# Zero regions of two gradients: stored from SBUF, or copied from memory to memory

## The chip, the cores and the metric

The kernel runs on one core of one Trainium2 chip. The metric is the device time of one execution in microseconds (us). Several executions are timed, and the median counts. Smaller is better.

## The reference

The reference is one step of a decoding layer and all of its gradients. With batch 4, one token, model width 512, it computes

- `xn = layernorm(x)`;
- attention of 32 query heads over 8 groups of cached keys and values. The cache has 4096 positions, and only the last `W = 1024` of them are used (`k_cache[:, :, Sk - W:, :]`);
- a feed-forward part of width 1792, `(gelu(xn @ w_gate) * (xn @ w_up)) @ w_down`;
- the output `x + attention + feed-forward`, and with `jax.vjp` the gradients for x, the two caches, and the five weight matrices, for a given `grad_out`.

The gradients of the two caches, `out_2` (keys) and `out_3` (values), have the caches' full shape, 4 x 8 x 4096 x 128 in bf16. The window leaves the first 3072 of the 4096 positions unused, so three quarters of these two outputs are zeros: 4 x 8 x 3072 x 128 x 2 bytes = 25.2 MB in each, 50.3 MB together. They must be written all the same.

## The kernel before, in words

The program is written for the engines in a fixed order: each engine runs its instructions as the source issues them. Almost all DMAs are issued by SP (`nc.sync`), in one queue. ACT issues one load at the start and the two small outputs at the end, and POOL issues the later weight loads.

*Stages.* First the small inputs are loaded, then the feed-forward weights, the first attention weights `wo` and `wq`, and the first blocks of keys (`kb`) and values (`vb`). The feed-forward part is computed and its weight gradients are made piece by piece. Then a loop over `t` runs through four stages (`NT = 4`), each with two groups of the cache. A stage transposes key and value blocks, forms scores and softmax (`kv_steps`, `softmax`), forms the softmax's gradient (`softmax_d`), multiplies back (`odq`), sums up (`fin`), and loads what the stage after the next one needs (`load_kv`, `load_w`).

*Pieces in the background.* The gradients of caches and weights are cut into short closures. They lie in a queue, `bg`, and `tick(n)` runs the next n of them between the steps of a stage. A piece of the cache gradients (`dvdk`) is one matmul and a copy from PSUM to a staging tile (`stg_dv`, `stg_dk`, three buffers). The last piece of a tile issues the tile's store and after that calls `zero()`. The pieces of the weight gradients stage in `osb_d`, `osb_g`, `osb_o` and `osb_q`, four buffers.

*Zeros.* `ztile` is an SBUF tile of 128 x 6144 bf16 that POOL fills with zeros at the start (L167). `zlist` lists 32 regions, 16 in each of the two outputs; a region is the unused part of two groups (`ZR = 2`) of one batch element, 2 x 768 KB = 1.573 MB. `zero(n)` takes the next n regions and stores `ztile` to each. Calls of `zero` are spread over the program: three at the start (L168), some with the feed-forward gradients, one after each cache gradient tile, four in the last stage, and what is left at the end.

*Stores.* All stores go through `store`, which declares that stores of the kinds "rest" and "zeros" write disjoint parts, so that no waits are made between them:

```
for k in ("rest", "zeros") if kind == "rest" else ("rest",):
    tc.declare_no_dep(d.ins, group=k, reason="stores write disjoint parts of the outputs")
tc.add_to_no_dep_group(kind, d.ins)
```

All the stores have one line in the profile, L103, and are told apart by their tiles. DMA completions use eight semaphores in turn, so a DMA on SP waits for the landing of the one issued eight places earlier.

Of the kernel before, what the change touches and what calls it, by code (L numbers as in the profile page):

```python
# [14 lines left out]
P = 128  # L15
# [3 lines left out]
def kernel(  # L19
# [28 lines left out]
    nc = tc.nc  # L48
# [7 lines left out]
    K0 = Sk - W  # L56
# [43 lines left out]
    def store(eng, out, in_, kind):  # L100

        eng.nop()
        d = eng.dma_start(out=out, in_=in_)  # L103
# [3 lines that stand above are left out]
        return d  # L107
# [48 lines left out]
    ZR = 2  # L156
    ZW = K0 * Dh * ZR // P
    ztile = const.tile([P, ZW], BF16, name="ztile")
    zlist = deque((og, b, g) for b in range(B) for g in range(0, G, ZR) for og in (out_2, out_3))

    def zero(n=1):
        for _ in range(min(n, len(zlist))):
            og, b, g = zlist.popleft()
            store(nc.sync, og[b, g:g + ZR, 0:K0, :].rearrange("g (m j) d -> m g (j d)", m=P // ZR), ztile[:], "zeros")


    nc.gpsimd.memset(ztile[:], 0.0)  # L167
    zero(3)  # L168
    ident_f = const.tile([P, P], FP32, name="ident_f")
    nc.vector.tensor_copy(out=ident_f[:], in_=ident[:])  # L170
# [304 lines left out]
    def dvdk(t, k):  # L475
        src, mr, og = st[t][("P", "dS")[k]], st[t][("do", "q")[k]], (out_3, out_2)[k]
        nm = ("dv", "dk")[k]

        def piece(g, j, held):
            if j == 0:  # L480
                held["stg"] = stage.tile([P, JB, Dh], BF16, name="stg_" + nm, tag="stg")
            stg = held["stg"]
            mps = ps_w.tile([P, NQ, Dh], FP32, name="kv_ps", tag="w")
            nc.tensor.matmul(mps[:].rearrange("p q d -> p (q d)"), lhsT=src[:, j * P:(j + 1) * P],  # L484
                             rhs=mr[:, g].rearrange("p q d -> p (q d)"), start=True, stop=True)
            evac(stg[:].rearrange("p (q j) d -> p j q d", q=NQ)[:, j], mps[:], 512)
            if j == JQ - 1:
                store(nc.sync, og[:, t * GP + g, K0:Sk, :].rearrange("b (m j) d -> m b (j d)", j=JB),
                      stg[:].rearrange("p j d -> p (j d)"), "rest")
                zero()  # L490

        made = []
        for g in range(GP):
            held = {}
            made.append([lambda g=g, j=j, held=held: piece(g, j, held) for j in range(JQ)])
        return made
# [158 lines left out]
    def piece_d(f4, i, n, held):  # L655
        if i == 0:
            held["osb"] = outp.tile([P, 4, D], BF16, name="osb_d", tag="o")
        m = n * P // 4
        mps = ps_w.tile([P, D], FP32, name="dwd_ps", tag="w")
        nc.tensor.matmul(mps[0:m], lhsT=a_s[:, f4].rearrange("p i f -> p (i f)")[:, i:n * P:4], rhs=dyr[:],  # L660
                         start=True, stop=True)
        evac(held["osb"][0:m, i, :], mps[0:m], 512)
        if i == 3:
            store(nc.sync, out_8[4 * f4 * P:(4 * f4 + n) * P, :].rearrange("(p i) n -> p (i n)", i=4),
                  held["osb"][0:m].rearrange("p i n -> p (i n)"), "rest")
            zero(f4 % 2)
# [151 lines left out]
```

## Time and profile before

| | |
|---|---|
| median of 3 runs | 282.77 us (282.73 to 283.42) |
| the profiled execution, its own time | 283.0 us |
| its span in the profile | 281.0 us |
| busy: PE, DVE, ACT, POOL | 203.1, 164.1, 117.8, 40.1 us |
| moved by DMA | 112.12 MB in 19565 packets |
| zero stores | 32 of 1536 KB, median 18.1 us from issue to landing |

The span is the time from the first to the last event of the profiled execution; its own time is somewhat longer, since it includes what lies around the span. PE is the matrix engine, DVE the vector engine, ACT the scalar engine; SPq is the queue of the engine that issues DMAs. A busy share belongs to the whole span, and stages differ. The time from issue to landing of a DMA includes the time that it stands in the queue behind others.

### The profile page before, as it was taken

How to read it: one execution, taken by the hardware profiler on the slowest of the kernel's cores; microseconds unless marked ns; L12 is line 12 of the kernel's file. 1: busy time of each engine (PE TensorE's matmuls, PEld its weight loads, DVE VectorE, ACT ScalarE, POOL GpSimd, SP SyncE). 2: the span in 40 equal slices, each digit the busy share in tenths (PEclk: the TensorE clock that was granted, in tenths of full speed). 3: DMA queues.
4: the chain of work that ended last, by engine and by line, in shares of the span. 5: the costliest groups of instructions: out<-in, count | busy, mean ns of one | idle time of the engine just before them, and what ended most of it. 6: DMA issues, size and time to landing. Idle time of an engine off the chain costs nothing.

```text
span 281.0 us, 6867 instructions
## 1 busy us (share of the span) xinstructions
PE 203.1 (72%) x2972; PEld 138.8 (49%) x2972; DVE 164.1 (58%) x313; ACT 117.8 (42%) x219; POOL 40.1 (14%) x40
## 2 busy tenths in 40 slices
PE   0276699959789889998999299898999599390000
PEld 0265476735456665566775156677556484140000
DVE  7946646645776655577666067767677728386000
ACT  2030386635035418764448056443866038370000
POOL 8600000007002150002250000223000400000000
PEclk9999589986999999999999969999999979977555
DMA  7999999999999999999999999999999999999990
GB/s 264 393 375 431 431 426 417 425 419 424 369 395 424 422 420 420 426 415 422 419 417 411 412 424 423 431 383 398 385 368 415 387 432 410 425 429 422 398 422 30
DMA packets 19565, 112.12 MB, mean 399 GB/s; under 512 B 1664, under 2 KB 4496, under 8 KB 11088
## 3 DMA queue, kind: packets, MB, share of 16 engines
q1 hardware_dynamic: 17744, 103.56, 89.6%
q0 software_dynamic: 1632, 6.29, 5.6%
q10 hardware_dynamic: 160, 1.84, 1.9%
q8 instruction: 23, 0.38, 0.5%
q14 instruction: 6, 0.05, 0.0%
HBM read 30.68 MB, written 81.01 MB: 397 GB/s over the span
## 4 chain that ended last, share of the span: by engine, by line
PE 47%; DMA 22%; DVE 16%; ACT 4%; issue 2%; SPq 0%; DVEq 0%; ACTq 0%
DMA out_dram<-stg_dv 13%; PE T_ps L279 8%; PE kv_ps L484 7%; DMA wd_sb<-in_B_w_down_dram 6%; PE S_ps L345 5%; PE od_ps L450 5%; DMA out_dram<-osb_g 4%; DVE T_sb L98 3%; DVE dS_s L367 2%; PE wdT_ps L279 2%; PE dwq_ps L520 2%; PE acc_ps L256 2%; PE dwd_ps L660 2%; DVE P_s L367 2%; PE wgT_ps L279 2%
## 5 line engine op out<-in xcount | busy, mean ns | idle before, releaser
L98 DVE COPY T_sb<-T_ps 128x1024 bf16<-128x1024 bf16 x64 | 44.1, 688 | 26.7 <-PE T_ps L279 26.5
L97 ACT CAST stg_dk<-kv_ps 128x512 bf16<-128x512 f32 x52 | 29.2, 588 | 31.2 <-PE kv_ps L484 12.4
L97 ACT CAST stg_dv<-kv_ps 128x512 bf16<-128x512 f32 x51 | 28.1, 588 | 24.9 <-PE kv_ps L484 24.3
L484 PE MATMUL kv_ps<-qmr,dS_s 128*128 128x512 bf16 x64 | 23.9, 414 | 11.3 <-ACT stg_dk L97 10.6
L463 POOL TENSOR_TENSOR o_s<-od_r,msk_r 128x512 bf16<-128x512 bf16 x8 | 9.1, 1157 | 110.2 <-DVE od_r L455 80.9
L484 PE MATMUL kv_ps<-domr,P_s 128*128 128x512 bf16 x64 | 21.3, 382 | 0.0
L279 PE MATMUL T_ps<-ident,vb 128*128 128x128 bf16 x256 | 20.3, 225 | 0.4 <-DVE T_sb L98 0.4
L279 PE MATMUL T_ps<-ident,kb 128*128 128x128 bf16 x256 | 20.4, 225 | 0.0
L279 PEld LDWEIGHTS <-kb 128*128 128x128 bf16 x256 | 17.5, 101 | 4.5 <-issue 1.3
L279 PEld LDWEIGHTS <-vb 128*128 128x128 bf16 x256 | 17.2, 101 | 5.0 <-issue 3.2
L97 ACT CAST osb_q<-dwq_ps 128x512 bf16<-128x512 f32 x25 | 14.6, 587 | 8.3 <-PE dwq_ps L520 7.4
L329 POOL TENSOR_TENSOR domr<-r,msk 128x1024 bf16<-128x1024 bf16 x4 | 7.6, 1892 | 71.2 <-DVE r L326 65.1
L97 ACT CAST osb_g<-dwg_ps 128x512 bf16<-128x512 f32 (+1 forms) x25 | 12.3, 544 | 12.3 <-PE dwg_ps L673 6.3
L97 ACT CAST osb_o<-dwo_ps 128x512 bf16<-128x512 f32 x24 | 13.9, 586 | 4.5 <-PE dwo_ps L505 2.9
L98 DVE CAST stg_dk<-kv_ps 128x512 bf16<-128x512 f32 x12 | 8.0, 688 | 12.0 <-DMA out_dram<-stg_dv 11.2
L98 DVE COPY wgT<-wgT_ps 128x1024 bf16<-128x1024 bf16 x14 | 9.6, 686 | 6.8 <-PE wgT_ps L279 6.8
L345 PE MATMUL S_ps<-T_sb,qm 128*32 128x256 bf16 x128 | 12.7, 387 | 0.6 <-DVE T_sb L98 0.5
L345 PE MATMUL S_ps<-T_sb,dom 128*32 128x256 bf16 x128 | 12.7, 388 | 0.1
L505 PE MATMUL dwo_ps<-dyr,o_s 128*128 128x512 bf16 x32 | 12.4, 413 | 0.3 <-ACT stg_dk L97 0.2
L98 DVE COPY woT<-woT_ps 128x1024 bf16<-128x1024 bf16 x16 | 11.0, 686 | 2.7 <-PE woT_ps L279 2.3
L484 PEld LDWEIGHTS <-dS_s 128*128 128x128 bf16 x64 | 6.2, 101 | 12.2 <-issue 11.1
L520 PE MATMUL dwq_ps<-od_r,xnm 128*128 128x256 bf16 x64 | 11.6, 274 | 0.3 <-ACT osb_q L97 0.2
(188 smaller groups left out, 385.0 us busy)
## 6 DMA issues: line engine op xcount, KB each, us to landing
out_dram<-ztile SPq DMA_DIRECT2D x32, 1536.0 KB, 18.1
kb<-in_A_k_cache_dram SPq DMA_DIRECT2D x8, 1024.0 KB, 17.4
vb<-in_A_v_cache_dram SPq DMA_DIRECT2D x8, 1024.0 KB, 20.7
out_dram<-stg_dv SPq DMA_DIRECT2D x8, 1024.0 KB, 13.0
out_dram<-stg_dk SPq DMA_DIRECT2D x8, 1024.0 KB, 20.8
out_dram<-osb_o SPq DMA_DIRECT2D x8, 512.0 KB, 17.4
out_dram<-osb_q SPq DMA_DIRECT2D x8, 512.0 KB, 13.8
out_dram<-osb_g SPq DMA_DIRECT2D x8, 448.0 KB, 14.3
```

The lines of the kernel that those rows point to most:

```text
L97: return nc.scalar.copy(out=out, in_=in_)
L98: return nc.vector.tensor_copy(out=out, in_=in_)
L256: nc.tensor.matmul(ps[:, c, :], lhsT=lf(c), rhs=rhs, start=(k == 0), stop=(k == len(terms) - 1))
L279: nc.tensor.transpose(ps[:, i, :], a, ident[:])
L329: nc.gpsimd.tensor_tensor(out=mr[:].rearrange("p g q d -> p (g q) d"), in0=r4[:, k, :].unsqueeze(1).broadcast_to([P, SL, Dh]), in1=msk[:]. ...
L345: nc.tensor.matmul(ps[b * RB:(b + 1) * RB, :], lhsT=zt[:, b * GP + g, c0:c0 + RB], rhs=T_sb[:].rearrange("p (x b) -> p b x", b=B)[:, b, :] ...
L367: nc.vector.scalar_tensor_tensor(out=out[:], in0=src[:].unsqueeze(2).broadcast_to([P, WQ, B]), scalar=rr[:, 0:1], in1=mskb[:].unsqueeze(1) ...
L450: nc.tensor.matmul(od_ps[g * 32:g * 32 + B * rep, k, g, :], lhsT=cols[:, jj, g * NQ + q, :], rhs=blks[(t, g)][:, j, :], start=(j == 0), st ...
L463: nc.gpsimd.tensor_tensor(out=o_s[:, g], in0=rows[:, g].unsqueeze(1).broadcast_to([P, rep, Dh]), in1=msk_r[:].unsqueeze(2).broadcast_to([P ...
L484: nc.tensor.matmul(mps[:].rearrange("p q d -> p (q d)"), lhsT=src[:, j * P:(j + 1) * P], rhs=mr[:, g].rearrange("p q d -> p (q d)"), start ...
L505: nc.tensor.matmul(mps[:], lhsT=o_s[:, g].rearrange("p r d -> p (r d)")[:, i:rep * Dh:rep], rhs=dyr[:], start=True, stop=True)
L520: nc.tensor.matmul(mps[:, i].rearrange("p g d -> p (g d)"), lhsT=xnm[:, i2 * 2 + i, c * P:(c + 1) * P], rhs=dq_r[:].rearrange("p g d -> p ...
```

## The change

The first three calls store `ztile` as before. Each of the other 29 regions is written by a DMA from memory to memory: its source is the first zero region, `out_2[0, 0:2, 0:3072, :]`, which the first of the three stores has filled. The copies are issued by SP in the places of the stores that they replace. A region is described as 16 x 2 rows of 24,576 bf16, 48 KB each, where a store has 64 x 2 rows of 6144, 12 KB each. As the copies read what the first store has written, the first of them gets a wait for that store's landing.

```diff
     zlist = deque((og, b, g) for b in range(B) for g in range(0, G, ZR) for og in (out_2, out_3))
+    ZN = len(zlist)
 
     def zero(n=1):
+
         for _ in range(min(n, len(zlist))):
             og, b, g = zlist.popleft()
-            store(nc.sync, og[b, g:g + ZR, 0:K0, :].rearrange("g (m j) d -> m g (j d)", m=P // ZR), ztile[:], "zeros")
+            dst = og[b, g:g + ZR, 0:K0, :]
+            if len(zlist) >= ZN - 3:
+                store(nc.sync, dst.rearrange("g (m j) d -> m g (j d)", m=P // ZR), ztile[:], "zeros")
+            else:
+                store(nc.sync, *(x.rearrange("g (m j) d -> m g (j d)", m=16) for x in (dst, out_2[0, 0:ZR, 0:K0, :])), "zeros")
```

## Prediction, made before the changed kernel ran

> **What bounds the kernel now.** I read the time slices first, then the queue rows, then windows without compute, then the chain.
>
> The slices of the page (each figure is 1/40 of the span, 7 us; DMA is the busy share of the 16 engines in tenths, GB/s what they moved):
>
> ```profile
> span 281.0 us, 6867 instructions
> ...
> DMA  7999999999999999999999999999999999999990
> GB/s 264 393 375 431 431 426 417 425 419 424 369 395 424 422 420 420 426 415 422 419 417 411 412 424 423 431 383 398 385 368 415 387 432 410 425 429 422 398 422 30
> DMA packets 19565, 112.12 MB, mean 399 GB/s; under 512 B 1664, under 2 KB 4496, under 8 KB 11088
> ## 3 DMA queue, kind: packets, MB, share of 16 engines
> q1 hardware_dynamic: 17744, 103.56, 89.6%
> q0 software_dynamic: 1632, 6.29, 5.6%
> ...
> HBM read 30.68 MB, written 81.01 MB: 397 GB/s over the span
> ```
>
> The DMA row is full from the second slice to the last but one and the rate is flat near 420 to 430 GB/s. PE is busy 72% of the span, DVE 58%. So the 16 DMA engines set the time, and engine gaps are mostly results of it. Two windows confirm this (busy us and counts per engine, then clock, DMA share, GB/s):
>
> ```profile
> 22.00:37.00 15.00, 9.95 (x157) 7.85 (x155) 9.31 (x24) 4.41 (x8) 0.00 (x0) 0.67 1.02 432
> ...
> 266.00:272.00 6.00, 0.00 (x0) 0.00 (x0) 0.00 (x0) 0.00 (x0) 0.00 (x0) 0.50 1.04 432
> ```
>
> The first holds loads of 8 KB rows and zero stores of 12 KB rows, the second the last zero stores, with no compute at all. Both give 432 GB/s: the same ceiling for reads from and writes to HBM, so it lies in what both share, the engines or the SBUF side. The chain of waits names the same resource: its largest line is a store's landing, and the largest single piece a stage buffer's store waiting in the DMA queue:
>
> ```profile
> DMA out_dram<-stg_dv 13%; PE T_ps L279 8%; PE kv_ps L484 7%; DMA wd_sb<-in_B_w_down_dram 6%; PE S_ps L345 5%; PE od_ps L450 5%; DMA out_dram<-osb_g 4%; DVE T_sb L98 3%; DVE dS_s L367 2%; PE wdT_ps L279 2%; PE dwq_ps L520 2%; PE acc_ps L256 2%; PE dwd_ps L660 2%; DVE P_s L367 2%; PE wgT_ps L279 2%
> ```
>
> In order of time (start, duration, what):
>
> ```profile
> 137.81 23.51 DMA out_dram<-stg_dv
> ```
>
> **Prices out of the queue rows.** q1 used 0.896 x 16 x 281.0 = 4,028 engine-us for 17,744 packets and 103.56 MB; q0 0.056 x 16 x 281.0 = 252 for 1,632 and 6.29 MB. Solved for a price per packet and one per byte: 12.8 ns and 36.7 ns per KB (27.2 GB/s per engine, 435 for 16). Rounding of q0's 5.6% leaves 9 to 17 ns per packet. A zero store has 128 rows of 12.288 KB, 8 per engine: 8 x (12.288 x 36.7 + 12.8) = **3.71 us** of all engines. 32 of them are 119 us of the span, 50.3 of 112.1 MB.
>
> **What the Trainium skill says.** (1) "DMA: Bandwidth & Descriptors", Where 436 GB/s comes from: 16 SBUF ports of 27.2 GB/s, and these ports are the bottleneck. The trace agrees in size: 432. A memory-to-memory copy doesn't use these ports. (2) "HBM Reference", Specifications (TRN2): a domain has about 716 GB/s, shared by two cores. A copy reads and writes each byte there, so it can't go over 358. The trace of before can't show it: its total is 397, each byte crossing HBM once. (3) "Collectives: The Full Stack", the section on the fold count: about 31 GB/s per engine, measured in ring copies between cores. No row of before tests it. (4) "DMA: Bandwidth & Descriptors", Queues, rings and completion order: each engine changes between queue rows only at packet ends. A packet of 48 KB thus holds up q0 longer than one of 12.
>
> **The change, part by part.**
>
> 1. *29 of 32 zero stores become copies.* The compiled order on SP's queue is the same, each copy in its store's place (16x2x24576 elements: 32 rows of 49.15 KB, two per engine, so still all 16 engines). Bytes over the engines don't change, 29 x 1.573 = 45.6 MB. HBM reads rise from 30.7 to 76.3 MB, all traffic at HBM from 111.7 to 157.3.
>    - *At the old engine rate* a copy takes 2 x (49.15 x 36.7 + 12.8) ns = 3.63 us, 0.08 less for 96 fewer packets: 29 x 0.077 = **-2.2 us** (-1.6 to -3.0 by the packet price).
>    - *At the domain's ceiling.* At 27.2 GB/s per engine it would draw 2 x 435 = 870 GB/s, more than 716. At 358 a copy takes 4.39 us: 29 x (4.39 - 3.71) = +19.9 us. I take 350, an estimate just below that ceiling[...]: 4.49 us, 29 x 0.78 = **+22.7 us**. Mixed traffic may cost more: at 300 GB/s it is 5.24 us, +44.5.
>    - *Cover.* The 16 engines may be apart, some in a copy while others move SBUF data; then HBM's demand averages out (157.3 MB / 716 = 220 us, below the span) and the loss shrinks. The trace shows how far apart: at the end the rate falls off within about 3 us, less than a copy lasts. So I count little cover; half of it would leave about +10.
>    As the DMA row has no idle slice, a longer copy isn't hidden; it goes in full to the end.
>
> 2. *The added wait.* The first copy now waits for the landing of the first zero store, its source. That was issued at 18.5 us and landed 21.8 later (the trace's answer on ztile for that issue), at 40.3; the copy's issue in before is at 40.8, behind two osb_d stores. I take 0, with 2 us as the bound if landing slips. Behind it on SP stand the osb_d and osb_g stores, for which ACT's next staging buffers wait; the DMA backlog (landings of 10 to 26 us for zero stores) covers such a slip. Later copies have the same one-semaphore waits as the stores they replace.
>
> 3. *Longer packets beside POOL's loads.* wo and wq for the next stages come on q0, 17 packets per engine and MB. A copy gives them 2 turns where a store gave 8. The first pair is issued at 67.6 and used from 88.3, landing after 13 to 22 us: tight, so PE may wait some us there. The later pairs (100.7 to 129.6, 142.5 to 179.0) have room. While PE waits, SP's backlog keeps the engines working: 0 taken, 3 us as the bound.
>
> 4. *SP's issue time.* A zero store took SP 0.66 us (median), one per 9 us. A copy describes 32 rows a side instead of 128: between 0.66 less and no gain, and nothing on the path since the queue is full. The first three stores, ztile and its memset stay. No other queue's order moves.
>
> Sum against the profiled execution (283.0 us, 2.0 around its span): 283.0 + 22.7 + 0 + 0 = 305.7. The median of the runs is 282.77, 0.2 below, so 305.5.
>
> **Rivals.**
> - *Engine rate kept (faster).* If HBM feeds both sides, or engines are well apart, only the packets count: 283 - 2 = 281. For it: HBM never showed a limit of its own. Against it: 870 of 716.
> - *The copy outruns the SBUF ports (faster).* Place: the 29 copies. At 31 GB/s per engine a copy takes 3.17 us, 29 x -0.54 = -15.7: 267. It decides from where a copy averages under 3.71 us, that is over 424 GB/s. For it: the ceiling of 432 may be the ports'. Against it: it needs 992 GB/s of HBM whenever all engines copy.
> - *Half rate (much slower).* If an engine can't read and write memory at once, 435 / 2 = 217: 7.25 us a copy, 29 x 3.54 = +103: 386. For it: no row shows both ends in HBM. Against it: the 31 GB/s of the skill.
> - *The rows don't stay long.* If the hardware cuts 48 KB rows to packets of 4 KB, there are 384 per copy, not 32: 29 x 352 x 12.8 ns / 16 = +8.2 on any of the above.
>
> **How the numbers follow.** HBM ceiling, 290 to 328: 0.55. Half rate or near it, above 328: 0.15. Mostly covered by engines apart, 282 to 290: 0.12, a third of it no change. Engine rate kept: 0.10. Outrun: 0.08. So faster by over 0.3% (0.85 us, about what can be told from no change) 0.18, within it 0.04, slower 0.78. Forecast 305.5. The range 278 to 352 leaves out most of the outrun case (0.07) and the slower part of half rate (0.10); its upper end is a copy rate of about 257 GB/s.
>
> **What would show it.** Right: 29 issues out_dram<-out_dram; HBM read near 76 MB; packets near 16,800; the slices sink in proportion to the copies in them, with DMA still at 9; the stretch after the last compute grows by some 1.5 us for its two copies. Engine rate kept: the last stretch stays at 432. Half rate: slices with copies near 250 to 300 and PE below 60%. Wrong altogether: idle slices in the DMA row, which would mean a wait (the first copy's, or PE's on wo near 88 us) and not a rate.

## The result and the profile after

The changed kernel takes **295.55 us** (median, 294.95 to 296.5) against 282.88 us for the kernel before in the same comparison (282.73 to 283.42): 12.7 us more, ratio 1.0447, 95% interval 1.0413 to 1.0482. The span of the profiled execution grew from 281.0 to 294.5 us.

The page of the changed kernel: slices (now 7.4 us each), queue rows and HBM line.

```profile
span 294.5 us, 6866 instructions
...
DMA  7999999999999999999999999999999999999892
GB/s 272 388 386 425 436 414 442 398 367 377 353 439 379 418 399 424 361 440 422 395 409 434 416 440 421 376 381 355 373 351 312 387 343 355 425 406 347 272 396 100
DMA packets 16781, 112.12 MB, mean 381 GB/s; under 512 B 1664, under 2 KB 4496, under 8 KB 11088
...
q1 hardware_dynamic: 14960, 103.56, 90.0%
...
HBM read 76.29 MB, written 81.01 MB: 534 GB/s over the span
```

The DMA row is as full as before. The same 112.12 MB went through the engines in 2,784 fewer packets, and it took them longer: the rate sinks to 312 to 390 in many slices. That is a lower rate, not a wait. The queue row gives the whole difference: q1's packets now took 0.900 x 16 x 294.5 = 4,241 engine-us where they took 4,028, that is 213 more, or 213 / 16 = **13.3 us** of all engines. The span grew by 13.5. The trace also records the start and the length of every packet. By these records 9.4 us of the growth lie in the zero regions' own packets; most of the rest, 3.1 us, lies in the packets of 8 KB, which took 329 ns in the mean instead of 317. So packets beside the copies became slower too.

Three windows of the changed kernel (busy us and counts of PE, PEld, DVE, ACT, POOL, then clock, DMA share, GB/s). The first lies ahead of the first copy, the second is the long middle part, the third lies after the last compute, where the final copies run:

```profile
22.00:37.00 15.00, 9.64 (x157) 7.46 (x155) 9.39 (x24) 4.49 (x8) 0.00 (x0) 0.64 1.02 430
...
42.00:280.00 238.00, 183.22 (x2588) 122.22 (x2585) 137.65 (x260) 105.50 (x201) 29.12 (x22) 0.91 1.00 388
...
274.00:285.00 11.00, 0.00 (x0) 0.00 (x0) 0.00 (x0) 0.00 (x0) 0.00 (x0) 0.50 0.97 340
```

The middle part of the kernel before, which ends earlier:

```profile
42.00:268.00 226.00, 179.75 (x2571) 119.62 (x2568) 136.63 (x259) 104.89 (x199) 29.12 (x22) 0.93 1.00 412
```

Ahead of the first copy nothing has changed (430 GB/s, 432 before). In the middle the kernel before moved 412 GB/s, now it is 388. In the tail it had 432, now 340, with the engines still busy 97% of the time. Engines that are as busy and move less have packets that take longer. Whether the engine itself is slower in a copy, or what it reads from and writes to, is for the experiments.

The loss doesn't lie evenly. Late in the program four zero regions are issued in a row (start, duration), as stores in the kernel before and as copies now:

```profile
219.74 4.40 SPq L103 DMA_DIRECT2D out_dram<-ztile  x4
...
225.40 2.94 SPq L103 DMA_DIRECT2D out_dram<-out_dram  x4
```

Up to there 19 copies had been issued and the changed kernel was 5.7 us behind, about 0.30 us per copy. At the end it was 13.5 us behind, so the last 10 copies, which mostly stand close to each other, go with 7.8 us, about 0.78 each. The packet records agree: copy packets that started from 80 to 210 us took 1.85 us in the mean, those from 210 us on 2.21.

The chain of waits passes the delay on through a larger share of DMA landings (39% of the span, 22% before):

```profile
DMA out_dram<-stg_dv 21%; DMA out_dram<-osb_o 9%; PE T_ps L285 6%; DMA wd_sb<-in_B_w_down_dram 5%; PE kv_ps L490 5%; DMA out_dram<-osb_g 4%; PE S_ps L351 4%; PE od_ps L456 4%; DVE T_sb L98 2%; PE dwq_ps L526 2%; PE wgT_ps L285 2%; PE dwd_ps L666 2%; PE wdT_ps L285 2%; PE dwg_ps L679 2%; PE acc_ps L262 1%
```

In the list of waits (us in total, times, longest) ACT stands longer before a staging tile whose last store hasn't landed, 16.1 us where it was 11.6:

```profile
ACT stg_dk L97 <- DMA out_dram<-stg_dv: 16.1, 2, 8.2
```

### The profile page after: what moved, and what is told of

It reads as the page before. It is cut to its first block, busy times and chain, and to the rows that moved or that the text cites. A ratio compares the mean times of both kernels' runs of the same rounds, so it can differ in the third digit from the quotient of the medians.

```text
span 294.5 us, 6866 instructions
## 1 busy us (share of the span) xinstructions
PE 206.2 (70%) x2972; PEld 141.1 (48%) x2972; DVE 164.5 (56%) x313; ACT 117.5 (40%) x219; POOL 40.1 (14%) x40
## 2 busy tenths in 40 slices
DMA packets 16781, 112.12 MB, mean 381 GB/s; under 512 B 1664, under 2 KB 4496, under 8 KB 11088
## 4 chain that ended last, share of the span: by engine, by line
DMA 39%; PE 35%; DVE 11%; ACT 3%; issue 2%; SPq 0%; DVEq 0%; ACTq 0%
DMA out_dram<-stg_dv 21%; DMA out_dram<-osb_o 9%; PE T_ps L285 6%; DMA wd_sb<-in_B_w_down_dram 5%; PE kv_ps L490 5%; DMA out_dram<-osb_g 4%; PE S_ps L351 4%; PE od_ps L456 4%; DVE T_sb L98 2%; PE dwq_ps L526 2%; PE wgT_ps L285 2%; PE dwd_ps L666 2%; PE wdT_ps L285 2%; PE dwg_ps L679 2%; PE acc_ps L262 1%
## 5 line engine op out<-in xcount | busy, mean ns | idle before, releaser
L97 ACT CAST stg_dk<-kv_ps 128x512 bf16<-128x512 f32 x52 | 28.9, 589 | 35.7 <-DMA out_dram<-stg_dv 16.1
L490 PE MATMUL kv_ps<-domr,P_s 128*128 128x512 bf16 x64 | 22.1, 393 | 2.8 <-DVE woT L98 1.8
L351 PE MATMUL S_ps<-T_sb,qm 128*32 128x256 bf16 x128 | 12.7, 387 | 0.6 <-DVE T_sb L98 0.5
L351 PE MATMUL S_ps<-T_sb,dom 128*32 128x256 bf16 x128 | 12.7, 387 | 0.1
L526 PE MATMUL dwq_ps<-od_r,xnm 128*128 128x256 bf16 x64 | 12.6, 301 | 0.1
```

What stands on the lines that cost most here:

```text
L97: return nc.scalar.copy(out=out, in_=in_)
L351: nc.tensor.matmul(ps[b * RB:(b + 1) * RB, :], lhsT=zt[:, b * GP + g, c0:c0 + RB], rhs=T_sb[:].rearrange("p (x b) -> p b x", b=B)[:, b, :] ...
L526: nc.tensor.matmul(mps[:, i].rearrange("p g d -> p (g d)"), lhsT=xnm[:, i2 * 2 + i, c * P:(c + 1) * P], rhs=dq_r[:].rearrange("p g d -> p ...
```

## The experiments

*The theory:* one core gets a limited supply from its HBM, reads and writes together. When all 16 engines copy at once they ask for twice their own rate, which is more than that; while some engines move SBUF data beside them, part of the loss is covered. *The rivals:* a copy costs each engine something by itself; the place of the source matters; one event (the added wait, a late weight load) costs the time; row length matters.

### Copies and stores alone

The isolated kernels keep only the filling of `ztile` and the DMAs of `zero`, called as `zero(32)`; everything else is left out. Each ran once, so their times have no interval, but the effects are several us and more.

All stores, none replaced:

```diff
-            if len(zlist) >= ZN - 3:
+            if True:
```

> Only the 32 zero stores from SBUF, back to back on SP; all other work is left out. Both theories: 32 x 3.71 = 118.7 us of data at some 430 GB/s plus a head (memset, first landing) and tail of about 15 us. This is the base for the isolated copies.

Three stores and 29 copies, as in the change:

> Only the 3 zero stores and the 29 copies, back to back on SP; all other work is left out. Theory (HBM's supply is the limit when all 16 engines copy, and in the full kernel about half of that loss is covered by engines that are apart): a copy alone costs more than the 4.2 us seen in the full kernel, near 4.5 us (350 GB/s), so some 22 us over the isolated stores. Rival (a copy has a fixed cost of its own, whatever stands beside it): the same 4.2 us as in the full kernel, some 13 us over the isolated stores.

Measured: 128.98 and **162.65 us**. The 29 copies cost 33.7 us more than stores, 1.16 each: a copy alone is dearer than in the full kernel (12.7 / 29 = 0.44), and dearer than I had expected (some 22 us over the stores). The windows of the two, stores first (POOL busy, clock, DMA share, GB/s):

```profile
20.00:110.00 90.00, 0.00 (x0) 1.00 1.01 424
```

```profile
20.00:150.00 130.00, 0.00 (x0) 1.00 1.00 325
```

With no other work and with full engines, stores run at 424 GB/s and copies at 325. A copy reads and writes each byte in HBM, so HBM then moves 650 GB/s.

### Fewer engines at a time

Each copy in two DMAs of 8 rows by 2:

```diff
-                store(nc.sync, *(x.rearrange(..., m=16) for x in (dst, ...)), "zeros")
+                for q in range(2):
+                    store(nc.sync, *(x.rearrange(..., m=16)[q * 8:q * 8 + 8] for x in (dst, ...)), "zeros")
```

> As the isolated copies, but each copy is cut into two DMAs of 8 rows by 2, so that each runs on 8 engines; all other work is left out. Theory (HBM's supply): 8 engines ask for 435 GB/s of HBM, well inside it, so each packet of 48 KB runs at the engine's own 1.82 us: 58 x 2 x 1.82 = 211 us for the copies, 217 GB/s. Rival (an engine loses time on each memory-to-memory row by itself): 2.1 to 2.3 us a packet, 244 to 267 us for the copies.

Measured: 233.69 us. Less the head and tail of the isolated stores (128.98 - 32 x 3.71 = 10.3) and three stores (11.1), 212.3 are the copies', where the theory said 211 and the rival 244 to 267.

```profile
40.00:200.00 160.00, 0.00 (x0) 1.00 0.50 216
```

Half of the engines are busy and move 216 GB/s: 27.0 each, the rate of an engine in the stores of the kernel before (432 / 16). So a memory-to-memory row has no price of its own here, in either direction: with eight engines copying an engine loses nothing, and it doesn't go beyond 27 GB/s though SBUF is at neither end. A packet of 48 KB took 1.815 us; with 16 engines it took 2.40 in the mean.

Twelve engines, by rows of 32 KB (`m=24`):

> Isolated copies (all other work left out) as 24 x 2 rows of 32 KB, so that only 12 of the 16 engines carry them. Theory (HBM's supply of some 646 GB/s): 12 engines ask for 12 x 2 x 27.1 = 650 GB/s, just what there is; each row runs near the engine's own 1.22 us and the total stays near the 162.65 us of 16 engines: 160 to 168 us. Rival (the loss is a share of each engine's own rate, or grows with the number of rows in flight): 4/3 of the copies' time, 200 us and more, or clearly less than the 16 engines' time.

Measured: 163.22 us; 16 engines had 162.65.

```profile
20.00:150.00 130.00, 0.00 (x0) 1.00 0.75 324
```

Twelve engines, each at its own full rate of 27.0 GB/s, move as much as sixteen. The last four add nothing: in a long run of copies the limit is outside of the engines. Whether it is the memory itself or the path to it, these runs don't tell apart; I call it HBM's supply.

### Another source

```diff
-(dst, out_2[0, 0:ZR, 0:K0, :])
+(dst, A_k_cache[b, g:g + ZR, 512:512 + K0, :])
```

> Isolated copies whose source is not the one zero region but another part of the key cache for each copy, shifted by 512 positions (128 KB) against its destination; the contents of the two outputs are thus not zeros, and all other work is left out. Theory (HBM's supply): no change, 160 to 165 us. Rival (the loss comes from reading the same 1.5 MB again and again, or from source and destination lying at the same place of a 2 MB grid): clearly faster, toward 134 us.

Measured: 162.67 us, to 0.02 us the same as with the one source. Neither reading one region 29 times nor the equal offsets of source and destination cost anything.

### The cover

Alternating stores and copies (`if len(zlist) >= ZN - 3 or len(zlist) % 2`: 15 copies, 17 stores):

> Isolated as before (all other work left out), but from the fourth region on every second one is a copy (15 copies, 17 stores from SBUF, alternating in SP's one queue). Theory (cover by engines that are apart: while some copy, others store, and HBM's demand averages to 1.5 x 427 = 640 GB/s, about the 646 that the isolated copies drew): nearly all of the loss of 1.16 us per copy goes, 129 to 137 us. Rival (a copy pays its 1.16 us wherever it stands): 128.98 + 15 x 1.16 = 146.4 us.

The same DMAs in two blocks (`if len(zlist) >= ZN - 17`):

> The 17 stores and 15 copies of the alternating isolated kernel in two blocks, all stores first and then all copies (all other work left out). Theory (in the alternating order the stores beside the copies cover half of the loss): the copies pay in full, 128.98 + 15 x 1.16 = 146 us, against 137.44 alternating. Rival (15 copies cost 0.56 us each in any order): 137 us.

Measured: **137.44 us** alternating and **146.56** in blocks. The blocks pay in full: (146.56 - 128.98) / 15 = 1.17 us per copy. Alternating, it is (137.44 - 128.98) / 15 = 0.56. The theory had nearly all of the loss gone, and half of it stayed. The page of the blocked kernel shows both rates side by side:

```profile
GB/s 0 0 435 435 414 401 435 435 435 421 414 414 435 435 435 418 411 421 435 380 435 258 394 244 407 217 435 231 407 231 407 244 380 272 421 244 367 272 407 27
```

The left half, the stores, stays at 401 to 435. In the right half the rate swings, as a 48 KB packet is counted in one slice; over 70 to 135 us it averages 330. The alternating kernel, in one window and in its slices:

```profile
20.00:125.00 105.00, 0.00 (x0) 1.00 0.99 405
...
GB/s 0 0 388 424 406 406 243 424 493 322 489 312 500 315 507 348 391 482 337 504 319 489 337 500 341 402 482 337 478 341 478 359 489 355 460 420 362 471 116 14
```

From 40 to 125 us it moved 412 to 414 GB/s, close to the 424 of stores, which is 0.2 us per copy. The rest of the 0.56 lies at the two ends: in the last 11 us the engines were busy for 51% of the time, and the last slices (471, 116, 14) show that they don't end together.

Besides the order, one thing differs between the two kernels: the alternating copies all go to `out_3`, those of the block to both outputs. That hardly matters, as the packets of the isolated copies took about 2.38 us into `out_3` and 2.43 into `out_2`. So it is the order.

*Are the engines apart?* That was my theory: a copy is cheap between stores since other engines are in a store at the same moment. The profile doesn't name a packet's engine, but the packet records show how many copy packets run at once, and they speak against this as the whole cause. In the alternating kernel, from the first copy to the end, 14 or more of them run together for 36% of the time, one or none for 31%, so the engines are in step more often than not. Even those that had 14 or more running took 2.00 us in the mean, where the isolated copies took 2.40 with all 16. What counts there is the place in a run of copies. In the blocked kernel the first copy behind the stores took 2.02 us a packet (its first 16 packets 1.83, nearly an engine's own pace, with all 16 engines copying), the second copy 2.30, and from the third on it was about 2.4. The isolated copies began with 2.10 and 2.28. In the alternating kernel each copy is the first behind a store, and its packets took 1.99. So a short run of copies pays less than a long one, even with all engines in it. Why the first copy of a run is cheaper is not shown by any run here. In the changed full kernel the number of copies at one moment counts as well: packets with fewer than 10 copy packets running took 1.88 us, those with 14 or more 2.19.

### Half of the copies in the full kernel

The same condition as in the alternating kernel, in the full kernel:

> Full kernel, every second zero region from the fourth on a copy (the 15 that lie in the values' gradient), the others stores from SBUF. Theory (each copy pays by HBM's supply, with the cover that its neighbours give): about half of the 12.7 us, or a little less as zero regions next to each other are now of both kinds: +4 to +6.6, 287 to 290 us. Rival (the cost is one event, such as the added wait or a late load, and not the copies): close to 295 or close to 283.

Measured: 286.59 us (286.47 to 287.23), ratio 1.0117, interval 1.01 to 1.0133. That is 3.4 us for 15 copies, 0.23 each, against 0.44 each with 29. It is no single event, since then half of the copies would bring all or nothing. It is less than I expected (4 to 6.6): with a store of zeros between any two copies no long run of copies comes about, and 0.23 is near the 0.2 from the middle of the alternating kernel.

### The length of rows

`m=P // ZR` (12 KB, 128 per copy) and `m=192` (4 KB, 384 per copy), in the full kernel:

> The full changed kernel with copy rows of 12 KB in place of 48 KB. Theory (HBM's supply plus a price per packet): 29 x 96 packets more at 12.8 ns over 16 engines, 2.2 us slower than the 48 KB copies: near 298 us. Rival (rows of 48 KB hold up the other queue and keep the engines in step): faster than the 48 KB copies, below 294 us.

> Full changed kernel with copy rows of 4 KB (384 per copy). Theory (the engines wait for HBM in a copy anyway, so most of a packet's price of 12.8 ns is hidden there): like the 12 KB rows, 292 to 298 us. Rival (the price per packet adds in full, as the sum of the prediction had it): 29 x 352 x 12.8 ns / 16 = 8.2 us over the 48 KB rows, near 304 us.

Measured: 293.46 us (ratio 1.0363, interval 1.0306 to 1.042) for 12 KB, 294.58 us (1.0402, 1.0367 to 1.0438) for 4 KB. My expectation of 298 for 12 KB was wrong. The 4 KB rows make 10,208 packets more than the 48 KB rows, and no cost of them can be seen:

```profile
DMA packets 26989, 112.12 MB, mean 383 GB/s; under 512 B 1664, under 2 KB 4496, under 8 KB 22224
```

The packet records say the same without the rest of the program: for 48 KB the copies' packets took about 2.02, 2.03 and 2.04 us in rows of 12, 48 and 4 KB, where at 12.8 ns a packet 4 KB rows should have taken 0.14 more than 48 KB rows. That the packet's price is hidden because the engine is held up by HBM anyway is the reading I give it. Whether 12 KB rows are really a little better than 48 KB isn't settled: the intervals touch, and the two were measured in different comparisons.

### Copies on another queue

```diff
-                store(nc.sync, *(x.rearrange(..., m=16) for x in (dst, ...)), "zeros")
+                store(nc.gpsimd, *(x.rearrange(..., m=P // ZR) for x in (dst, ...)), "zeros")
```

> Full kernel, the 29 copies issued by POOL in rows of 12 KB, so that each engine can alternate between copy packets and SP's packets. Theory (cover by mixing): the loss by HBM's supply shrinks from some 12 us to below 5; but SP's stores no longer queue behind zeros, and POOL issues copies only as far as its own work lets it, so what is left for the end counts: 283 to 292 us. Rival (order doesn't matter, each copy has its price): 293 us or more.

The control issues the same 29 regions from POOL as stores of `ztile`:

> Control for the copies on POOL: the kernel before with 29 zero stores from SBUF issued by POOL. Theory: the same bytes at the same engine rate, 282 to 287 us; the difference of the POOL copies to this kernel is the price of memory-to-memory alone in mixed traffic, below 5 us. Rival: that difference is 10 us or more, as in SP's queue.

Measured: 302.56 us (ratio 1.0668, interval 1.0625 to 1.071) and 290.25 us (1.0252, 1.0222 to 1.0282). Both miss what I expected, and the rivals came true: the zeros on POOL cost 7 us by themselves, and the copies on top cost 12.3, as in SP's queue (12.7). The slices of the POOL copies show that this was no clean test:

```profile
DMA  7999999997999999999999999968799999999995
GB/s 276 383 388 430 436 420 370 365 378 318 320 408 414 397 374 393 422 422 408 408 408 356 413 426 426 384 198 319 241 412 371 392 379 340 339 368 408 410 418 201
```

There are slices where the engines are not full, at 198 to 319 GB/s: POOL issues zeros where its own program lets it, in bunches (seven from 210.8 us on, six from 243.2), and has none to give in between. The control differs in one more way: its first five stores were issued on POOL from 11.3 us on, the first five copies from 37.7, as POOL waited for the landing of their source. Still, mixing gained nothing that can be seen: for 48 KB the packets of the copies took about 2.06 us, no less than the 2.03 in SP's queue. No run here beat the kernel before.

## Why the prediction was right, point by point

I forecast 305.5 us, slower, with HBM's supply as the likeliest case (290 to 328), and 295.55 is in it. The direction and mechanism hold; the sum's terms do not all have their size.

- **The bound.** Right: the DMA engines were the limit, had no idle slices, and a slower copy went to the end in full. 13.3 us of added packet time stand against 13.5 of span.
- **The supply term, +22.7 at 350 GB/s.** Too small. Copies alone ran at 325 GB/s, 1.16 us more than a store instead of 0.78: 29 x 1.16 = 33.7 us. The figure of the Trainium skill ("HBM Reference", Specifications (TRN2), about 716 GB/s a domain) set the ceiling at 358; what a long run of copies drew was 650 of 716 GB/s, 91% of it, where I had deducted 2%. Nor is it a ceiling at each moment: the first 16 packets of the block of copies took 1.83 us, which is 430 GB/s copied, for some 2 us. For the domain's other core, which was idle here, nothing is shown.
- **The cover, put at nothing in the sum.** This is the step that failed. Of the 33.7 us only 12.7 arrived, so 62% was covered. I took the fall of the rate at the end, about 3 us, as the measure of how far engines are apart and concluded that this was too short. In the alternating kernel the engines do stay close, and a copy between stores is cheap all the same. Cover didn't need engines that are far apart; it was enough there that no long run of copies forms.
- **The sum.** It came out only 10 us too high because these two errors had opposite signs, and that is luck: with the copy's true price and no cover it would have been 282.8 + 33.7 = 316.5. The direction doesn't hang on this luck.
- **The packets, -2.2.** This stood in the case of the old engine rate and not in the sum. It was not seen: rows of 48, 12 and 4 KB lie within 2.1 us, in no order. The price of 12.8 ns didn't show in copies of all 16 engines.
- **The added wait, 0.** Right. The first store landed at 18.5 + 19.3 = 37.8 us, the first copy was issued at 41.9, behind an osb_d store that waited for ACT. The 21.8 us that I had read for the first store's landing belong to the second, issued at 19.6.
- **POOL's loads, 0.** Right: they landed in a median of 15.1 (wo) and 21.6 us (wq), wq 2.5 later than before, and PE shows no wait for them in the window from 86 to 100 us, where the first pair is used.
- **The tail.** I expected 1.5 us more after the last compute, for two copies. From the issue of dx_b to the end of the span it was 281.0 - 257.9 = 23.1 us and is now 294.5 - 268.5 = 26.0, so 2.9. Three copies are issued there, not two: one zero region went out at 251.6 us before and goes out at 269.8 now. That is 0.97 each, nearer to the 1.16 of copies alone than to the 0.44 of the whole kernel, which fits that they stand close together with little else left to move.
- **The rivals.** Half rate falls with 27.0 GB/s per engine at 8 engines. Outrunning the ports falls by the same number; the 31 GB/s that I had taken for it isn't reached here. Engine rate kept falls with the 325 GB/s of 16 engines. The Trainium skill ("DMA: Bandwidth & Descriptors", Where 436 GB/s comes from) has the ports as the bottleneck. These runs don't show that it is the ports alone: without SBUF at either end an engine keeps the same 27 GB/s. The last one, that rows don't stay long, falls with the 16,781 packets of the page.

## What to carry to other kernels

A transfer from memory to memory isn't free of the engines' limit, and it counts twice at HBM: before replacing a store from SBUF by a copy, add both sides at full engine rate and compare with what HBM gives. If DMA is the bound, the loss goes into the time, less what the order of the queue saves: here copies with other traffic between them cost 0.2 to 0.3 us, and long runs of them 1.16. So measure a transfer alone and mixed before pricing it, and where copies must be, keep them apart. A price per packet taken from one regime need not hold where another limit sets the pace.

## What the runs showed of the hardware

One core drew 650 GB/s from HBM in long runs of copies (2 x 325), with 12 engines and with 16 alike. A copy on 8 engines ran at 27.0 GB/s per engine, the rate of a store from SBUF. Alternating with stores in one queue, a copy lost 0.56 us instead of 1.17, and only 0.2 away from the ends of the kernel. In a block of copies behind stores the first copy took 2.02 us a packet, the third and later ones about 2.4. I had expected neither that the order within one queue would be worth half of the loss, nor that twelve times as many copy packets would bring no cost to be seen.
